# Transposing one granule's averages by DMA instead of TensorE, with an output tile moved ahead of its first FFN matmul

## Chip, cores, metric

One core of a Trainium2 chip. The metric is the device time of one execution in microseconds (us); a run is one such execution. The span of a profile is about 1.8 us shorter than the time of the same run.

## The reference, cut to what matters

```python
def _attn_ref(q, k, v, n_global, n_local):         # 4 batches, 8 heads, 768 tokens, 64 wide
    scores = scale * np.matmul(q, k.transpose(0, 1, 3, 2))
    keep = is_global | is_local                    # 8 global keys, a band of 96
    ...                                            # bias by distance, mask, softmax
    return np.matmul(a, v)

def _moe_ref(x, w_in, w_out, s, b):                # x: 3072 x 512, d_ff = 2048
    h = x @ w_in
    r = np.maximum(h, 0.0)
    g = s * (r * r) + b
    return g @ w_out

x = attn_out.transpose(0, 2, 1, 3).reshape(B * S, H * D)   # attention feeds the FFN
```

## The kernel before

The 3072 tokens are cut into 12 granules of 256. For each, attention gives the averages `xn` (tokens on partitions). They have to be transposed to `xT` (features on partitions) before the FFN's first product (L632 in the profile) can take them. After ReLU (ScalarE) and square (VectorE) the second product (L680, or for later granules the cheaper L968 and L832) gives the output. Everything is interleaved by hand in "steps": a step computes the score products of the next two units (L444; a unit is two heads of one granule), then the value products of its own two units (L504), with pieces of FFN work in between, so that TensorE has something to do while ScalarE and VectorE make the exponentials.

There are two ways to transpose the averages. Granules 0 to 3 use the first one, the others the second:

```python
    QK_PE = 4
    X_PE = 4
...
    def x_by_pe(j, evac=(nc.vector.tensor_copy, nc.scalar.copy)):
        t = xT_tile(j)
        nk = KC // len(evac)
        for e, ev in enumerate(evac):
            ps = ps_h.tile([P, nk, GT], BF16, name="ps_x", tag="psh")
            for kc in range(nk):
                for i in range(GB):
                    c = (e * nk + kc) * P
                    nc.tensor.transpose(          # L604: 8 for a granule
                        ps[:, kc, i * P : (i + 1) * P], xn[j][:, i, c : c + P], ident_bf[:]
                    )
            ev(t[:, e * nk : (e + 1) * nk, :], ps[:])     # L607: 2 copies from PSUM

    def x_by_dma(j):
        t = xT_tile(j)
        for i in range(GB):                       # L612: 2 for a granule, on SyncE's queue
            nc.sync.dma_start_transpose(t[:, :, i * P : (i + 1) * P], xn[j][:, i, :])
...
    def finish_granule(j):
        if j < X_PE:
            x_by_pe(j)
        else:
            x_by_dma(j)
        while stores:
            stores.pop(0)()
        if 6 <= j + LEAD < NJ:                    # later loads wait until this granule is done
            hold_loads(xT[j][0:1, 0, GT - 1 : GT])
            load_granule(j + LEAD)
```

Queries and keys of the granules from 4 on are also transposed by DMA (L363, four transposes of 128x512 a granule) on the same queue. The keys shifted by one block (`ko`) are copied from them by VectorE (L386, L387). The part of the order that the change touches:

```python
    qk_by_dma(5)                                  # granule 5's four transposes
    r0, q0 = p1_mm(2, 5)
    r0()
    stage_A(14)                                   # last values of granule 3
    stage_A(15, ps_h)
    q0()
    make_koff(4)                                  # the copies L386, L387
    run(p1[2][6:8])
    finish_granule(3)                             # the transposes in question
    run(scores(8))
    make_voff(4)
    p2_mm(2, 0, 0, FC // 2)
    emit_bvec()
    ...
    step(8, [lambda: rest(2, 0)] + late_p1(3, (0,)), late_p1(3, (1, 2)), late_p1(3, (3,)))
    step(
        9,
        [weight_sums[1]] + p2[2][1:2],
        [sg_sum(3)] + act_p1(3, (4, 5)),
        late_p1(3, (6,)) + [weight_sums[2]] + late_p1(3, (7,)) + [flush, sg_sum(1)],
    )
```

`late_p1(3, ...)` are pairs of FFN matmul groups of granule 3 (8 matmuls, then a ReLU, a square later); `rest` and `p2[2]` are granule 2's output tiles.

The softmax here doesn't subtract the row's maximum and nothing guards it: scores larger than these inputs give would overflow.

## Time and profile before

| before | value |
|---|---|
| time, median of the first 3 runs | 207.85 us (207.68 to 207.97) |
| span of the profile | 206.1 us |
| TensorE busy | 201.6 us |
| eight transposes of granule 3 (L604) | 0.45 us on TensorE |
| their copies out of PSUM (L607) | 0.42 us on VectorE, 0.58 us on ScalarE |

TensorE has hardly a gap, so the row to keep in mind is the 0.45 us: it is all that the change can gain. The lines of the profile that carry this are in the prediction.

### The profile page before, as it was taken

How to read it: one execution, taken by the hardware profiler on the slowest of the kernel's cores; microseconds unless marked ns; L12 is line 12 of the kernel's file. 1: busy time of each engine (PE TensorE's matmuls, PEld its weight loads, DVE VectorE, ACT ScalarE, POOL GpSimd, SP SyncE). 2: the span in 40 equal slices, each digit the busy share in tenths (PEclk: the TensorE clock that was granted, in tenths of full speed). 3: DMA queues.
4: the chain of work that ended last, by engine and by line, in shares of the span. 5: the costliest groups of instructions: out<-in, count | busy, mean ns of one | idle time of the engine just before them, and what ended most of it. 6: DMA issues, size and time to landing. Idle time of an engine off the chain costs nothing.

```text
span 206.1 us, 5375 instructions
## 1 busy us (share of the span) xinstructions
PE 201.6 (98%) x2209; PEld 162.5 (79%) x2214; DVE 164.8 (80%) x347; ACT 129.3 (63%) x200; POOL 70.2 (34%) x90
## 2 busy tenths in 40 slices
PE   8999999999999999999999999999999999999993
PEld 2678885557876588888888898888888889888883
DVE  6877689979989999999699865699866696737974
ACT  5767669585975668885763694763694754476200
POOL 8986333899555601808301908200000000000000
PEclk9999999999999999999999999999999999999999
DMA  5999999999999999999999999994360300340006
GB/s 156 177 178 201 207 206 180 155 153 131 126 143 125 156 125 229 117 168 188 145 272 192 131 173 202 180 192 78 54 207 3 101 4 0 69 138 0 3 7 197
DMA packets 110836, 28.17 MB, mean 137 GB/s; under 512 B 97852, under 2 KB 109308, under 8 KB 110812
## 3 DMA queue, kind: packets, MB, share of 16 engines
q0 software_dynamic: 76000, 13.11, 87.9%
q1 hardware_dynamic: 33612, 14.13, 39.9%
q10 hardware_dynamic: 1200, 0.59, 1.1%
q8 instruction: 17, 0.28, 0.5%
q14 instruction: 7, 0.06, 0.1%
HBM read 27.26 MB, written 6.29 MB: 163 GB/s over the span
## 4 chain that ended last, share of the span: by engine, by line
PE 95%; DMA 2%; DVE 0%; ACT 0%; issue 0%
PE ps L632 41%; PE ps L832 24%; PE ps L680 10%; PE ps_s L444 6%; PE ps_av L504 5%; PE ps L968 3%; DMA first<-in_k_dram 2%; PE ps_s L530 1%; PE ps_t L354 1%; PE ps_s L419 1%; PE ps_x L604 1%; PE ps_s L545 1%; PE ps_t L331 1%; PE ps_av L571 1%; PE ps_t L344 0%; PE ps_last L832 0%
## 5 line engine op out<-in xcount | busy, mean ns | idle before, releaser
L632 PE MATMUL ps<-xT,w_in_bf 128*128 128x256 bf16 x768 | 90.4, 273 | 0.0
L642 ACT ACTIVATE gT<-ps 128x512 bf16<-128x512 f32 x96 | 55.8, 598 | 46.0 <-PE ps L632 45.8
L632 PEld LDWEIGHTS <-w_in_bf 128*128 128x128 bf16 x768 | 73.0, 98 | 9.2 <-DVE xT L607 0.2
L453 ACT ACTIVATE pt<-ps_s 128x1024 bf16<-128x1024 f32 (+1 forms) x44 | 39.3, 946 | 2.9 <-PE ps_s L444 2.8
L832 PEld LDWEIGHTS <-gsum 128*128 128x128 bf16 x256 | 24.2, 98 | 3.7 <-DVE gsum L795 0.5
L460 DVE TENSOR_TENSOR pt<-pt,tmpl 128x1024 bf16<-128x1024 bf16 (+1 forms) x40 | 24.4, 644 | 2.1 <-ACT pt L453 2.0
L108 POOL DMA_DIRECT2D vb<-in_v_dram x24 | 21.6, 914 | 5.3 <-DMA w_out_bf<-in_moe_w_out_dram 3.3
L806 DVE TENSOR_TENSOR gT<-gT 128x1024 bf16<-128x1024 bf16 x20 | 13.7, 687 | 11.6 <-ACT gT L642 11.6
L680 PE MATMUL ps<-w_out_bf,gT 128*128 128x512 bf16 x91 | 21.8, 379 | 0.3
L469 DVE TENSOR_TENSOR xn<-ps_av,rc 128x256 bf16<-128x256 f32 x48 | 20.4, 425 | 1.7
L832 PEld LDWEIGHTS <-gT 128*128 128x128 bf16 x200 | 18.6, 98 | 2.3
L504 PEld LDWEIGHTS <-pt 128*128 128x128 bf16 x320 | 14.4, 97 | 2.8 <-DVE xn L469 0.9
L680 PEld LDWEIGHTS <-gT 128*128 128x128 bf16 x96 | 8.9, 98 | 9.6
L468 DVE RECIPROCAL rc<-ps_av 128x4 f32<-128x4 f32 x48 | 8.6, 179 | 9.1 <-PE ps_av L504 7.8
L504 PE MATMUL ps_av<-vb,pt 128*128 128x65 bf16 x208 | 15.5, 193 | 0.0
L832 PE MATMUL ps<-w_out_bf,gsum 128*128 128x256 bf16 x128 | 15.3, 273 | 0.0
L832 PE MATMUL ps<-wsub,gsum 128*128 128x256 bf16 x128 | 15.1, 273 | 0.0
L116 POOL DMA_DIRECT2D nat<-in_q_dram x14 | 12.5, 890 | 6.9 <-DMA nat<-in_q_dram 2.9
L645 DVE TENSOR_TENSOR gT<-gT 128x512 bf16<-128x512 bf16 x30 | 12.2, 421 | 3.2 <-ACT gT L642 2.7
L122 POOL COPY gate<-xT 1x1 bf16<-1x1 bf16 x6 | 1.9, 314 | 36.1 <-DMA xT<-xn 36.1
L116 POOL DMA_DIRECT2D nat<-in_k_dram x14 | 12.6, 900 | 4.7 <-DMA w_in_bf<-in_moe_w_in_dram 2.5
L832 PE MATMUL ps<-w_out_bf,gT 128*128 128x256 bf16 x120 | 13.9, 273 | 0.0
(124 smaller groups left out, 249.7 us busy)
## 6 DMA issues: line engine op xcount, KB each, us to landing
out_dram<-o_q SPq DMA_DIRECT2D x15, 256.0 KB, 2.6
vb<-in_v_dram POOLq DMA_DIRECT2D x24, 128.0 KB, 7.6
nat<-in_k_dram POOLq DMA_DIRECT2D x22, 128.0 KB, 6.8
nat<-in_q_dram POOLq DMA_DIRECT2D x22, 128.0 KB, 6.9
w_out_bf<-in_moe_w_out_dram POOLq DMA_DIRECT2D x4, 512.0 KB, 16.1
w_in_bf<-in_moe_w_in_dram POOLq DMA_DIRECT2D x4, 256.0 KB, 7.6
w_in_bf<-in_moe_w_in_dram POOLq DMA_DIRECT2D x2, 512.0 KB, 11.1
out_dram<-o_sb SPq DMA_DIRECT2D x4, 256.0 KB
```

Of the source, the lines that this page charges most:

```text
L108: nc.gpsimd.dma_start(vbuf[b % 2][:, sb, :, 0:D], rows_of(v, b, sb))
L116: nc.gpsimd.dma_start(t[:, n, i, :, :], rows_of(srcs[n], b, sb))
L444: nc.tensor.matmul(ps[:, hi, oc * P : (oc + 1) * P], lhsT=kt[rows], rhs=qt[rows], start=not bias, stop=not bias or part * GB + n == len(pl ...
L453: nc.scalar.activation(pt[:, :, 0:ncol], ps[:, :, 0:ncol], ACT.Exp, scale=QSCALE)
L460: nc.vector.tensor_tensor(pv, pv, m.rearrange("p h a c -> p h (a c)"), ALU.mult)
L469: nc.vector.tensor_tensor(dst, av[:, :, :, 0:D], rc[:].to_broadcast((P, 2, 2, D)), ALU.mult)
L504: nc.tensor.matmul(av[:, i, hi, 0 : D + 1], lhsT=pt[:, hi, c * P : (c + 1) * P], rhs=vv, start=(n == 0), stop=(n == len(terms) - 1),)
L632: nc.tensor.matmul(ps[:, i, :], lhsT=w_in_bf[:, kc, fc * P : (fc + 1) * P], rhs=xT[j][:, kc, :], start=(kc == 0), stop=(kc == KC - 1),)
L642: nc.scalar.activation(gs, ps[:], ACT.Relu)
L680: nc.tensor.matmul(po[:], lhsT=g_of(j)[:, fc, tb * P : (tb + 1) * P], rhs=w_out_bf[:, fc, :], start=(fc == 0), stop=(fc == FC - 1),)
L806: outs.append(lambda: nc.vector.tensor_tensor(gs, gs, gs, ALU.mult))
L832: nc.tensor.matmul(ps[:, tb, cs], lhsT=stat[:, fc, tb * P : (tb + 1) * P], rhs=mov[:, fc, cs], start=(fc == 0), stop=(fc == NH - 1),)
```

## The change

The intent: take granule 3's transposes off TensorE, which bounds the kernel, and leave them to the DMA engines. As a DMA transpose takes longer to arrive, the work that doesn't need it (all of granule 2's output) is moved ahead of granule 3's first FFN matmul.

```diff
-    X_PE = 4
+    X_PE = 3
@@ finish_granule
-            hold_loads(xT[j][0:1, 0, GT - 1 : GT])
+            hold_loads(g_of(2)[0:1, FC - 1, GT - 1 : GT] if j == 3 else xT[j][0:1, 0, GT - 1 : GT])
@@ steps 8 and 9
-    step(8, [lambda: rest(2, 0)] + late_p1(3, (0,)), late_p1(3, (1, 2)), late_p1(3, (3,)))
+    step(8, [lambda: rest(2, 0)], [lambda: p2_mm(2, 1, 0, FC // 2)], [lambda: rest(2, 1)])
     step(
         9,
-        [weight_sums[1]] + p2[2][1:2],
-        [sg_sum(3)] + act_p1(3, (4, 5)),
-        late_p1(3, (6,)) + [weight_sums[2]] + late_p1(3, (7,)) + [flush, sg_sum(1)],
+        late_p1(3, (0, 1)),
+        [weight_sums[2]] + late_p1(3, (2, 3)),
+        act_p1(3, (4, 5)) + [flush, sg_sum(3)] + late_p1(3, (6,)) + [weight_sums[1]] + late_p1(3, (7,)) + [flush, sg_sum(1)],
     )
```

The rest of the diff only joins two lines of step 10.

More of the change, by code (lines that the diff above doesn't have):

```diff
@@ L1285 @@
         [bias_diff, lambda: shifted_template(range(H)), sg_prod(5)],
-        [sg_sum(4)],
-        pre=[sg_sum(2)],
+        [sg_sum(4)], pre=[sg_sum(2)],
     )
```

## The prediction

> **What bounds the kernel now.** I read the page's first part, its slices and its chain first.
>
> ```profile
> span 206.1 us, 5375 instructions
> ...
> PE 201.6 (98%) x2209; PEld 162.5 (79%) x2214; DVE 164.8 (80%) x347; ACT 129.3 (63%) x200; POOL 70.2 (34%) x90
> ...
> DMA  5999999999999999999999999994360300340006
> ...
> PE 95%; DMA 2%; DVE 0%; ACT 0%; issue 0%
> ```
>
> TensorE is busy for 98% of the span and carries 95% of the chain that ended last. Nothing else holds the end. So work taken off TensorE shortens the run by its full length, and any new wait of TensorE lengthens it by its full length. The DMA row is the second thing to see: the DMA engines are at 9 tenths from the second slice (5 us each) to the 27th, so a transfer added at 60 us joins a full system.
>
> Then I read the chain in order of time around the change:
>
> ```profile
> 57.23 1.75 PE ps L632 x16
> 58.98 0.45 PE ps_x L604 x8
> 59.42 0.55 PE ps_s L444 x16
> 59.98 0.32 PE ps L680
> ...
> 67.73 0.87 PE ps L632 x8
> 68.61 0.55 PE ps_s L444 x16
> ```
>
> Columns: start, length, what. The eight transposes of granule 3 (L604) hold TensorE for 0.45 us; right after come the score products of step 8 (L444) and granule 2's output (L680).
>
> What the transposes' neighbour waits for is in the timeline of VectorE and of the weight loads:
>
> ```profile
> 59.24 0.18 DVE L387 COPY ko<-kx 128x64 bf16<-128x64 bf16 x1
> ...
> 59.54 0.27 PEld L444 LDWEIGHTS <-ko 64*128 64x128 bf16 x8
> ```
>
> The shifted keys ko of granule 4 are finished at 59.42, and the second half of L444 loads them at 59.54. There is only 0.12 us of slack between the two. The last transposed queries of granule 4 are just as close: issued at 49.34, 9.8 us to landing in the DMA view of that window, so there at 59.14, and L444 starts at about 59.36.
>
> Last, the issuing queue (SyncE) and what its transposes get from the DMA engines:
>
> ```profile
> 52.70 2.10 SPq L363 DMA_TRANSPOSE kx<-nat  x1
> 54.90 1.34 SPq L363 DMA_TRANSPOSE qx<-nat  x1
> 56.34 1.59 SPq L363 DMA_TRANSPOSE kx<-nat  x1
> 58.02 1.81 SPq L363 DMA_TRANSPOSE qx<-nat  x1
> 66.28 1.19 SPq L363 DMA_TRANSPOSE kx<-nat  x1
> ```
>
> Granule 5's four transposes are issued until 59.83, then the queue is free until 66.28: the hole that the new transposes will use. The DMA view of two windows (58.2 to 65.9, then 65.9 to 70.5) shows when those four move:
>
> ```profile
> q0 software_dynamic: 3712, 0.47, 121.0%
> q1 hardware_dynamic: 2283, 0.53, 57.8%
> ```
>
> ```profile
> q0 software_dynamic: 5606, 0.71, 241.3%
> ...
> q1 hardware_dynamic: 3, 0.00, 0.1%
> ```
>
> Columns: packets, MB, share. In the first window queue 1 carries about 4 x 512 packets of 256 bytes and the completion packets; in the second it is empty. So the four transposes, though issued from 52.70 on, move from 58.2 to 65.9, 1.93 us each, and the queue's work is done at 65.9.
>
> **What the Trainium skill says.** "TensorE: Matmul & The Clock Gate", Part 4: PE-mode transpose: it is a matmul whose output goes to PSUM, so a copy must follow; about 275 ns each in a kernel. The trace agrees on the copies (L607: 0.42 us on VectorE, 0.58 us on ScalarE), but eight in a row cost 0.45 us, 56 ns each, as they are pipelined; I use 0.45. "DMA: Bandwidth & Descriptors", SWDGE vs HWDGE vs iDMA: software and hardware queues feed different rings of each DMA engine, which takes them in turn. The trace agrees: from 59 to 63 us queue 0 moved 1794 packets and queue 1 1537, close to one for one, so a transpose has at most half of a busy engine's turns. Same page, Rules for kernel authors: issue a DMA early and wait for it late. That is what moving granule 2's output forward tries; the question is whether the distance suffices. "TensorE: Matmul & The Clock Gate", Why this matters for your kernels: idle gaps of more than about 3 us cost clock. The clock row of this trace is full throughout; the wait I expect is shorter, so I count no loss of clock.
>
> **The change part by part.** *Removed:* eight transposes, 0.45 us of TensorE on the path; two copies off the path. *Added:* two DMA transposes of granule 3's averages. The averages are ready at 58.37 (the last normalisation, 57.95 + 0.42), the queue is free at 59.83, so I expect the issues at 59.9 and about 61.2. *Moved:* the other half of granule 2's output (16 matmuls of 128x512) goes ahead of granule 3's first FFN matmul, so four FFN pairs that used to lie between now come later. No work is added, and the changes from one kind of matmul to another stay about as many. *Gate:* the loads of granule 7 wait for the last square of granule 2 (60.08 in this trace) in place of xT. The gate's copy ran at 61.75 only because the POOL queue reached it then, so nothing changes.
>
> Step 1, the saving at once. L444 could start at 58.98, but its queries land at 59.14 and ko is still finished at 59.42, as VectorE does that ahead of the copy that goes. With 0.06 us for the signal the second half of L444 starts at about 59.48 in place of 59.54 to 59.59. So of the 0.45 us only about 0.1 is left; the rest becomes a wait for ko and the queries. After L444 TensorE is at 59.90.
>
> Step 2, TensorE's arrival at granule 3's first FFN matmul. From 59.90: half an output tile 1.83, the bias vector 0.44, scores 0.55, the tile's other half 1.83, values (L504) 0.24, 1.75, 0.24, 1.75, scores 0.55, each as the chain has it. Sum 9.18, so 69.08. The same work of before, counted without moving anything, would stand at 59.42 + 0.55 + 9.18 = 69.15.
>
> Step 3, the landing of xT. Behind granule 5's transposes the two can move from 65.9. At the best pace (queue 1 moved 384 packets per us from 59 to 63, some 540 per transpose: 1.4 us) they end at 68.7, at the mean pace with its pauses (1.93 us) at 69.8. To the landing I add 0.8: granule 5's first two landed at 52.70 + 8.6 = 61.3 and 54.90 + 7.6 = 62.5, and by equal shares they ended at 60.1 and 62.1. So xT is there between 69.5 and 70.6; centre 70.0. Both blocks are needed, since the matmul takes 256 tokens.
>
> Step 4, the net. The FFN of granule 3 starts at 70.0 in place of the 69.15 that equals the pace of before: +0.85 us. The wait on TensorE itself is 0.9 us.
>
> Step 5, step 9 is denser. All eight FFN pairs of granule 3 fall in one step of about 8 us: ScalarE has eight evacuations of 0.60, two squares of 0.63 and two exponentials of 0.96 there, 8.0 us; VectorE has six squares, two weight differences of 1.21, a sum of 0.68, two normalisations of 0.6. The last squares, the sum for product 1 and 5, and the next masks end later relative to TensorE than now, and already now the values of unit 21 wait for the average before them (0.37 us at 81.09 in place of 0.24). I give 0.2 us for this, chosen low because TensorE's wait lets both engines catch up.
>
> Sum: +0.85 + 0.2 = +1.05 us on 207.85. Weighted with the case that xT is in time (below), I predict **208.7 us**.
>
> **The rivals.** *A: xT is in time.* Then the change is worth step 1's 0.1 us to at best 0.45 us: 207.4 to 207.8. For it: xT of granule 4 lands in 4.9 and 4.1 us, and from 59.9 and 61.2 that would be 66. Against: those two found the queue empty and the loads ending; at 60 us the transposes of granule 5 are ahead, with 8.6 and 7.6 us to landing. I give it 25%. *B: a long wait.* From the issue at 66.28 to the first packet of that transpose at about 70.5 the queue was empty and still took 4 us. If xT's descriptors come that slowly, or a pause as at 63.5 to 64.4 (10 GB/s) falls in, xT lands at 71 to 72: 209.7 to 210.5. I give it 15%. *C: the delay spreads.* Granule 6's loads and transposes go through the same engines, 1.5 us later at most; its queries landed at 78.8 and are needed at 81.5, so 2.7 us of slack and no new wait. *D: VectorE or ScalarE becomes the bound in step 9.* Step 5 made larger: up to 0.6 us, 208.5 even with xT in time.
>
> **Range and chances.** From 207.5 (A) to 209.9 (start of B). The three runs of before lie within 0.3 us, so noise is small. Faster by 2% would need 4.2 us and only 0.45 is removed; slower by 2% would need a wait of over 4 us. Faster 0.01, same 0.97, slower 0.02.
>
> **What would show it.** Right: SyncE issues two xT transposes at about 60 and 61; they land near 70; the first L632 of granule 3 follows a gap of about 0.9 us on TensorE whose releaser is the DMA of xT; L444 of step 8 starts hardly earlier than now, its second half bound by ko. Wrong: no gap ahead of L632 (step 3 fails, rival A); L444 a full 0.45 us earlier (step 1 fails); or a gap at the products after step 9 that is larger than the one ahead of L632 (step 5 and rival D).

## The result, and the profile after

| | median, us | range, us | runs |
|---|---|---|---|
| before | 207.78 | 207.67 to 207.97 | 6 |
| after | 209.28 | 208.42 to 210.08 | 6 |

The ratio is 1.0069 (95% interval 1.0043 to 1.0094): 0.7% slower, "same" at the 2% line. A ratio here is the mean time of one kernel's fast runs over that of the other's of the same rounds, so it is not quite the ratio of the medians. Two things stand out. The loss of 1.50 us by medians is more than all that could be gained. And the changed kernel's runs are spread over 1.66 us, where those of before lie within 0.30 us. The profile happens to be of its slowest run (210.08 us), which has to be remembered when its waits are read.

The page of the changed kernel (summary, chain and the group of the FFN's first product):

```profile
span 208.3 us, 5362 instructions
...
PE 201.6 (97%) x2201; PEld 161.9 (78%) x2206; DVE 164.9 (79%) x346; ACT 128.8 (62%) x199; POOL 70.2 (34%) x90
...
PE 82%; DMA 6%; DVE 5%; ACT 4%; SPq 1%; issue 1%
...
L632 PE MATMUL ps<-xT,w_in_bf 128*128 128x256 bf16 x768 | 90.1, 273 | 1.5 <-DMA xT<-xn 1.5
```

The eight matmuls are gone from the count (2209 to 2201), but the span is 2.2 us longer. TensorE's share of the chain that ended last fell from 95% to 82%, and the last line says for what: L632 waited 1.5 us for the DMA of xT. That column was 0.0 before. The chain in order of time (start, length, what) shows the path:

```profile
59.52 0.19 DVE ko L387
...
59.76 0.42 PE ps_s L444 x8
60.17 1.32 SPq L612
...
61.54 9.16 DMA xT<-xn
...
70.75 1.92 PE ps L632 x16
...
81.10 1.20 DVE pt L460 x2
...
82.43 0.44 DVE xn L469
...
82.91 0.41 PE ps_av L504 x8
```

There are three new places where something other than TensorE sets the pace: the shifted keys ko at 59.7, the landing of xT at 70.70 (9.16 us after the start of its second issue, at 61.54; the chain counts a DMA from there), and VectorE's normalisation ahead of unit 21's values at 82.9. SyncE's timeline shows the queue that xT shares:

```profile
52.41 1.32 SPq L363 DMA_TRANSPOSE kx<-nat  x1
...
58.10 1.96 SPq L363 DMA_TRANSPOSE qx<-nat  x1
60.16 4.01 SPq L612 DMA_TRANSPOSE xT<-xn  x2
```

Granule 5's transposes are issued up to 60.06 and xT's follow at once; between them there is no room. The DMA view of 66.1 to 69.6 us (packets, MB, share) shows xT's own passage (q1), with the load queue (q0, GpSimd's loads) beside it:

```profile
q0 software_dynamic: 2131, 0.27, 119.5%
q1 hardware_dynamic: 1096, 0.26, 60.8%
```

Two transposes are 1024 packets of 256 bytes; they took the 3.5 us of this window, about 1.75 us each.

**Where the 2.2 us are.** A table by stage can be read off TensorE's timeline at four marks: (a) the start of the 16 L632 just ahead of granule 3's transposes (57.07 before, 57.08 after), (b) the first L680 after step 8's scores (59.91, 60.08), (c) the first L444 of step 10 (76.63, 78.32), (d) the first L632 of granule 4 (82.72, 84.58); then to the end of VectorE's last result (203.26, 205.11) and from there to the end of the span. The stages hold the same TensorE work in both, but for the eight transposes in a to b. I use the same marks for the experiments.

| stage, us | before | after | difference |
|---|---|---|---|
| a to b: last transposes, step 8's scores | 2.84 | 3.00 | +0.16 |
| b to c: granule 2's output, granule 3's FFN | 16.72 | 18.24 | +1.52 |
| c to d: step 10 | 6.09 | 6.26 | +0.17 |
| d to VectorE's last result | 120.54 | 120.53 | 0.0 |
| from there to the end | 2.84 | 3.19 | +0.35 |

The sum is 2.2 us, the difference of the spans. Stage a to b is the one that should have become 0.45 us shorter. Why it did not is seen where VectorE and GpSimd are listed together, before:

```profile
58.07 0.88 POOL L108 DMA_DIRECT2D vb<-in_v_dram  x1
...
58.62 0.58 DVE L386 COPY ko<-kx 128x1024 bf16<-128x1024 bf16 x1
```

and after:

```profile
58.38 0.87 POOL L108 DMA_DIRECT2D vb<-in_v_dram  x1 [0.90 <-DMA vb<-in_v_dram]
...
58.63 0.85 DVE L386 COPY ko<-kx 128x1024 bf16<-128x1024 bf16 x1
```

The same copy started at the same time, but took 0.85 in place of 0.58 us, and in both it ended 0.23 to 0.25 us after GpSimd had finished writing a load's descriptors; the same copy with nothing beside it (at 57.25 in run 10) takes 0.42 us. The Trainium skill, "SBUF — State Buffer", SBUF: two separate sides, says that VectorE in its fast mode and GpSimd share a port pair under an exclusive lock for a whole instruction (that this copy runs in that mode is not shown here). The three durations agree with that, if the lock is taken and let go some 0.2 us after GpSimd's recorded start and end: at 66.78 in the changed kernel the next such copy started only 0.19 us after a write's recorded start, took 0.42 us, and it was the write that was longer (1.08 us). As GpSimd's loads are not timed against this copy, its end is a matter of chance.

The last stage, +0.35 us, is far from everything that was changed. SyncE's own waits show a difference there, before:

```profile
SPq L1383 <- DMA out_dram<-o_last: 0.6, 2, 0.3
...
SPq L1383 <- DMA out_dram<-o_q: 0.4, 1, 0.4
```

and after:

```profile
SPq L1382 <- DMA out_dram<-o_last: 1.4, 2, 1.3
```

(total, times, longest). The last stores themselves land after the same 1.9 us in both. At the end of the kernel SyncE waits one after another, in a fixed order, for the completion semaphores (the counters by which a DMA tells that it has landed). Those that SyncE's and ScalarE's DMAs carry are given out in turn, so with two more DMAs, xT's, the last stores carry other ones. The packed trace names them: before, the last store had the semaphore that is waited for last (118), and the waits ended with its landing; after, it has an early one (103), and six more waits of 0.06 us each follow its landing. That is 0.36 us.

### The profile page after: what moved, and what is told of

It reads as the page before. It is cut to its first block, busy times and chain, and to the rows that moved or that the text cites. A ratio compares the mean times of both kernels' runs of the same rounds, so it can differ in the third digit from the quotient of the medians.

```text
span 208.3 us, 5362 instructions
## 1 busy us (share of the span) xinstructions
PE 201.6 (97%) x2201; PEld 161.9 (78%) x2206; DVE 164.9 (79%) x346; ACT 128.8 (62%) x199; POOL 70.2 (34%) x90
## 4 chain that ended last, share of the span: by engine, by line
PE 82%; DMA 6%; DVE 5%; ACT 4%; SPq 1%; issue 1%
PE ps L632 36%; PE ps L832 24%; PE ps L680 7%; PE ps_av L504 4%; DMA xT<-xn 4%; PE ps_s L444 4%; DMA first<-in_k_dram 2%; ACT gT L642 2%; PE ps L968 1%; ACT pt L453 1%; DVE xn L469 1%; DVE pt L460 1%; PE ps_s L419 1%; DVE gT L645 1%; PE ps_s L530 1%; PE ps_t L354 1%
## 5 line engine op out<-in xcount | busy, mean ns | idle before, releaser
L632 PE MATMUL ps<-xT,w_in_bf 128*128 128x256 bf16 x768 | 90.1, 273 | 1.5 <-DMA xT<-xn 1.5
L632 PEld LDWEIGHTS <-w_in_bf 128*128 128x128 bf16 x768 | 73.1, 98 | 10.6 <-DMA xT<-xn 1.6
L680 PE MATMUL ps<-w_out_bf,gT 128*128 128x512 bf16 x91 | 21.8, 379 | 0.3
L504 PEld LDWEIGHTS <-pt 128*128 128x128 bf16 x320 | 14.4, 98 | 3.1 <-DVE xn L469 1.1
L680 PEld LDWEIGHTS <-gT 128*128 128x128 bf16 x96 | 8.8, 98 | 9.3
L504 PE MATMUL ps_av<-vb,pt 128*128 128x65 bf16 x208 | 15.4, 193 | 0.1
L122 POOL COPY gate<-xT 1x1 bf16<-1x1 bf16 x5 | 1.4, 282 | 36.4 <-DMA xT<-xn 36.4
```

The source lines that it names most:

```text
L504: nc.tensor.matmul(av[:, i, hi, 0 : D + 1], lhsT=pt[:, hi, c * P : (c + 1) * P], rhs=vv, start=(n == 0), stop=(n == len(terms) - 1),)
L632: nc.tensor.matmul(ps[:, i, :], lhsT=w_in_bf[:, kc, fc * P : (fc + 1) * P], rhs=xT[j][:, kc, :], start=(kc == 0), stop=(kc == KC - 1),)
L680: nc.tensor.matmul(po[:], lhsT=g_of(j)[:, fc, tb * P : (tb + 1) * P], rhs=w_out_bf[:, fc, :], start=(fc == 0), stop=(fc == FC - 1),)
```

## The experiments

The theory after the result: (T) moving the transposes to the queue puts xT behind granule 5's four, which themselves go at half pace beside the loads, and TensorE arrives before it; the order by itself is nearly free. The rivals: (O) the new order costs it, as the FFN of granule 3 is packed into one step and VectorE falls behind; (L) the latency of a DMA transpose costs it, whatever is ahead of it in the queue.

All kernels gave correct results. Times are medians, with range and number of runs; the ratio is against the kernel before in the same rounds (whose medians were 207.68, 207.80, 207.83 and 207.78 in the four batches). Against the changed kernel's interval of 1.0043 to 1.0094, those of runs 1, 7 and 9 lie wholly below. Those of 4, 5, 8 and 10 overlap it, so their gains on it are differences of medians that the times alone do not make sure. Landing times below are the last updates of xT's completion semaphores in the packed traces.

### 1. The new order alone

```diff
# against the changed kernel
-    X_PE = 3
+    X_PE = 4
```

> The new order alone, granule 3's averages still transposed on TensorE. Theory (the loss is TensorE's wait for the DMA transposes): no DMA wait is left, so 207.8 to 208.1 us, at most 0.3 us over the kernel before for the denser step 9. Rival (the new order itself costs, as eight FFN pairs crowd ScalarE and VectorE in one step): 209 us or more, close to the changed kernel's 209.28.

Measured: 207.96 us (207.73 to 208.17, 5), ratio 1.0010 (0.9998 to 1.0022). The profile has no wait for a DMA in steps 8 to 10; stages a to b and b to c are 2.84 and 16.72 us, exactly those of before. Only step 10 is longer, 6.56 us, in the slowest of its runs. So O is worth some 0.3 us of the 1.5. The end of the kernel is as before too (2.85 us from VectorE's last result).

### 2. The transposes by DMA in the old order

```diff
# against the kernel before
-    X_PE = 4
+    X_PE = 3
```

> The DMA transposes alone, in the old order, where granule 3's first FFN matmul stands at about 64.5 us. Theory (xT lands at about 70 us whatever TensorE does, set by the transposes ahead of it in the queue): TensorE waits 5 to 6 us there and nothing gives it back, 213 to 214 us. Rival (landing follows the issue by 4 to 5 us as for granule 4's xT, so at 65 to 66 us): 208.5 to 209.5 us.

Measured: 215.72 us (214.60 to 216.19, 4), ratio 1.0376 (1.0348 to 1.0405): slower. TensorE's timeline, and the row of granted clock on the page:

```profile
69.43 1.89 PE L632 MATMUL ps<-xT,w_in_bf 128*128 128x256 bf16 x8 [5.12 <-DMA xT<-xn]
```

```profile
PEclk9999999999998599999999999999999999999999
```

TensorE came to granule 3's FFN 5.12 us before xT did, yet xT landed at 69.38, no later than in the changed kernel (70.70). So its landing does not depend on when it's wanted. The move of granule 2's output is worth 6.4 us (215.72 - 209.28), the loss of clock included: without it the change would be a clear loss. The time was 2 us above what I expected: the clock fell to 8 and 5 tenths in two slices, the mean to 0.984, and eight L632 took 1.89 us, where the other kernels need 1.04. The wait of 1.45 us in the changed kernel left its clock at 9 throughout. This agrees with the limit that the prediction quotes from the Trainium skill.

### 3. The two scalar loads taken out of the queue at the start

Ahead of granule 5's transposes, the queue also carries s and b, broadcast to 128 partitions: 256 packets of four bytes. In the changed kernel's DMA view, 57.4 to 58.7 us, queue 1 shows

```profile
q1 hardware_dynamic: 512, 0.05, 62.4%
```

512 packets but only 0.05 MB: by size, half of them are these. They hold the queue for about 1 us (by the trace's packet records 57.5 to 58.6).

```diff
+    load_scalars()          # right after the first FFN groups, at the program's start
...
     qk_by_dma(4)
-    load_scalars()
```

> The changed kernel with the loads of the two scalars s and b issued before granule 4's transposes instead of between those of granules 4 and 5: their 256 packets of 4 bytes leave the queue ahead of the transposes. Theory (one queue worked off in order, a packet per turn): at 384 packets per us they hold it 0.7 us, so xT lands 0.5 to 1 us earlier and the run takes 208.4 to 208.8 us. Rival (a fixed latency from issue to landing, or the pace of issuing): no change, 209.3 us.

Measured: 209.52 us (208.82 to 210.92, 6), ratio 1.0094. A miss by the experiment's own fault: the small packets now came among the first loads; L504 waited 0.57 us for the first values at 11.29, and mark a stands at 57.74 in place of 57.08. Its profile shows no wait for xT, but as two things changed at once it decides nothing. Run 7 repeats it in a better place.

### 4. Granule 5's transposes taken off the queue

The four transposes that stand ahead of xT are done by TensorE instead. It costs 16 TensorE transposes, twice what the change saved.

```diff
-    qk_by_dma(5)
     r0, q0 = p1_mm(2, 5)
...
-    step(8, [lambda: rest(2, 0)], [lambda: p2_mm(2, 1, 0, FC // 2)], [lambda: rest(2, 1)])
+    step(
+        8,
+        [lambda: rest(2, 0), lambda: qk_wide(5, 0, cp)],
+        [lambda: p2_mm(2, 1, 0, FC // 2), lambda: qk_wide(5, 1, acp)],
+        [lambda: rest(2, 1)],
+    )
```

> The changed kernel with granule 5's keys and queries transposed on TensorE in step 8 (16 transposes, 0.9 us more TensorE work) instead of by DMA ahead of xT in the queue. Theory (xT waits behind granule 5's transposes): xT lands at 64 to 66 us, before it is needed, the wait of 0.9 to 1.5 us goes and 0.9 us of work comes: 208.5 to 208.9 us, faster than the changed kernel in spite of more work on the bound engine. Rival (the wait is not due to the queue, or the order costs): 209.8 to 210.3 us.

Measured: 208.67 us (208.65 to 208.85, 5), ratio 1.0047 (1.0035 to 1.0059). SyncE's timeline:

```profile
58.16 2.52 SPq L612 DMA_TRANSPOSE xT<-xn  x2
```

xT's packets moved from 62.5 to 66.4 by the trace's records, xT landed at 67.77 (later than the 64 to 66 expected), and L632 started at 69.60 with no wait. With more work on TensorE, this kernel's median is 0.6 us below the changed one's, and its runs lie within 0.2 us where those lay within 1.66. So the four transposes ahead are what made xT late, and the times scatter less without them. But L is not refuted. The DMA view of 58.5 to 62.4 us has nothing on queue 1:

```profile
q0 software_dynamic: 4684, 0.59, 240.0%
q8 instruction: 1, 0.02, 2.1%
```

On this empty queue xT's first packet still came 4.3 us after the start of its first issue (58.16), and the two transposes landed 7.4 and 8.4 us after the starts of theirs, where the changed kernel has 8.9 and 9.2. (That is beside a full load queue; at 162.42, with no load moving, a transpose of xT lands after 2.4 us in the same kernel.) The second one landed 2.93 us earlier than there. Of this, 2.14 us is that SyncE, without the four issues before it, could issue it earlier (59.40 in place of 61.54), and 0.79 us that it took less time from there. Stage b to c is 17.61 us, 0.89 above before: the 16 transposes and nothing else.

### 5. More work put ahead of xT

Both value groups of step 9 (L504, 0.5 us) come ahead of granule 3's FFN.

```diff
     step(
         9,
-        late_p1(3, (0, 1)),
-        [weight_sums[2]] + late_p1(3, (2, 3)),
-        act_p1(3, (4, 5)) + ...
+        [],
+        [],
+        late_p1(3, (0, 1)) + [flush, weight_sums[2]] + late_p1(3, (2, 3)) + [flush] + act_p1(3, (4, 5)) + ...
+        pool=ps_h,
     )
```

> The changed kernel with both value products of step 9 (L504, 0.48 us) ahead of granule 3's first FFN matmul. Theory (xT lands at a time of its own; every microsecond of other work ahead of it is hidden): the wait falls by 0.4 to 0.5 us: 208.7 to 209.0 us. Rival (the wait moves along with TensorE's order): no change, 209.3 us.

Measured: 208.84 us (208.16 to 209.43, 6), ratio 1.0043 (1.0021 to 1.0064): as expected. In the profiled run, the second longest, L632 started at 70.07 after a wait of 0.43 us for xT. The landing near 70 again, and less waiting before it: 0.5 us of work put ahead of the landing took 0.44 us off the loss, by medians of different batches. (The edit also moves the points where squares are flushed and takes another PSUM pool.)

### 6. The scalars on another queue (and two kernels built on it)

```diff
     def load_scalars():
-        nc.sync.dma_start(s_bc[:], moe_s.to_broadcast((P, 1)))
-        nc.sync.dma_start(b_bc[:], moe_b.to_broadcast((P, 1)))
+        nc.scalar.dma_start(s_bc[:], moe_s.to_broadcast((P, 1)))
+        nc.scalar.dma_start(b_bc[:], moe_b.to_broadcast((P, 1)))
...
     template(range(H))
+    load_scalars()
...
     qk_by_dma(4)
-    load_scalars()
```

> The changed kernel with the loads of the two scalars issued at about 30 us from ScalarE's queue, so that neither the start of the kernel (as in the run with early scalars, whose first values then came 0.6 us late) nor the transposes' queue has their packets. Theory (the queue is worked off in order, its 256 packets of 4 bytes took a turn each at 57.5 to 58.6 us): granule 5's transposes and xT move 0.7 to 1 us earlier, TensorE's wait for xT falls by as much: 208.3 to 208.7 us. Rival (pace or latency of issuing): 209.3 us.

Together with the edit of run 5 and VectorE's weight difference moved to step 8:

> Scalars off the queue, value products first, and one weight difference (1.2 us of VectorE) moved from the dense step 9 into step 8. Theory: xT's wait of 0.5 to 1.5 us is covered (1.2 us gained), and the wait of unit 21's values for the average before them (0.43 us in the run with the order alone) goes: 207.6 to 207.9 us, as the kernel before. Rival: still over 208.5 us.

And with the copy of the shifted keys earlier as well:

> The same, and granule 4's shifted keys ko copied ahead of granule 3's last averages instead of behind them, so that step 8's score products no longer wait for them. Theory (most of the 0.45 us saved was turned into a wait for ko): 0.2 to 0.3 us faster than without this, 207.3 to 207.6 us, the first version under the kernel before. Rival (the queries of granule 4, landing at about 59.1 us, hold it as much): no gain.

Measured: 225.83 us (225.16 to 226.35, 5), 226.18 us (225.71 to 226.60, 4) and 226.32 us (226.09 to 227.14, 4); ratios 1.086 to 1.089. All three share one fault, which ScalarE's timeline of the first shows:

```profile
53.27 1.04 ACT L253 COPY tmpl<-tmpl 128x1024 bf16<-128x1024 bf16 x1 [17.78 <-DMA kx<-nat]
```

The second scalar load, issued from ScalarE, was given a completion semaphore that a transpose of granule 4 was using, so its issue (52.73) and all of ScalarE stood still for 17.78 us until that transpose had landed. These three say nothing on the question, except how dear a shared completion semaphore can be (and something on the kernel's end, below).

### 7. The scalars on the same queue, but at 30 us

Now they stay on SyncE's queue, but are issued where it is empty. A memset of their tiles by VectorE keeps them from going earlier.

```diff
     run(p1[0][7:8])
+    nc.vector.memset(s_bc[:], 0.0)
+    nc.vector.memset(b_bc[:], 0.0)
+    load_scalars()
...
     qk_by_dma(4)
-    load_scalars()
```

> Third try at taking the scalars' 256 packets out from between the transposes: SyncE issues them alone at about 28 us (they wait for a small fill of their tiles), after the start and long before granule 4's transposes, and no other engine's queue is involved. Theory (queue worked off in order): granule 5's transposes and xT move 0.7 to 1 us earlier, the wait for xT falls by as much: 208.3 to 208.7 us. Rival (pace or latency of issuing): 209.3 us.

Measured: 208.39 us (208.08 to 208.80, 5), ratio 1.0027 (1.0015 to 1.0040): as expected, and 0.9 us less than the changed kernel (209.28 in an earlier batch). By the trace's packet records xT's last packet left at 67.8 in place of 69.5; xT landed at 68.45, and L632 started at 69.07 with no wait. Stage b to c is 16.77, against 16.72 before. So the loss in that stage (1.52 us in the changed kernel's profile) was the wait for xT, and what stands ahead of xT made it. The edit takes the two loads out of the queue and their issues, 0.6 us each, off SyncE, so that xT's issue starts at 59.31 in place of 60.16; this run does not tell these two apart.

What is left in this profile: a to b is 3.02 (a wait for the last queries, 0.23 us, where the saving should be), c to d is 6.60 (unit 21's values wait 0.46 us for VectorE), and the end is 3.17.

### 8. Scalars early, values first, and a weight difference moved

```diff
# scal_sp, with run 5's edit, weight_sums[1] taken out of step 9, and
-    step(8, [lambda: rest(2, 0)], [lambda: p2_mm(2, 1, 0, FC // 2)], [lambda: rest(2, 1)])
+    step(8, [lambda: rest(2, 0)], [lambda: p2_mm(2, 1, 0, FC // 2), weight_sums[1]], [lambda: rest(2, 1)])
```

> Scalars as in the run just named, value products of step 9 first (these alone gave 208.84), and one weight difference of VectorE moved out of the dense step. Theory: the wait for xT is covered and the one for unit 21's average gone: 207.6 to 207.9 us, as the kernel before. Rival: over 208.4 us.

Measured: 208.60 us (208.34 to 209.06, 5), ratio 1.0044 (1.0031 to 1.0057). A miss, no faster than run 7. TensorE's timeline shows two waits for VectorE in place of those removed:

```profile
59.55 0.40 PE L444 MATMUL ps_s<-qx,ko 64*128 64x128 bf16 x8 [0.44 <-DVE ko L387]
...
73.73 3.65 PE L632 MATMUL ps<-xT,w_in_bf 128*128 128x256 bf16 x32 [0.33 <-DVE xn L469]
```

### 9. The shifted keys earlier too

```diff
# the kernel of run 8, and
     qk_by_dma(5)
+    make_koff(4)
     r0, q0 = p1_mm(2, 5)
...
     q0()
-    make_koff(4)
```

> The same, and granule 4's shifted keys copied ahead of granule 3's last averages. Theory (most of the 0.45 us saved had turned into a wait for ko): 0.2 to 0.3 us faster than without, 207.3 to 207.6 us, under the kernel before. Rival (granule 4's last queries hold step 8's scores as much): no gain.

Measured: 208.16 us (208.06 to 208.79, 6), ratio 1.0027 (1.0014 to 1.0040). It misses what I expected, but is 0.44 us faster than run 8. Stage a to b is 2.40 us, 0.44 less than before: here, for the first time, the whole gain of the eight transposes shows. So the prediction's step 1 had the right cause. (Of the two medians alone this can't be said: the intervals of runs 8 and 9 overlap.) The copy now started 0.13 us ahead of GpSimd's descriptors and took 0.42 us, and the small one after it took 0.53 us (0.18 elsewhere), ending with GpSimd's (58.22 and 58.24), as the lock would have it. But TensorE now comes earlier to an xT that is not earlier: in its longest, profiled run L632 at 69.94 waited 0.63 us for it.

### 10. The same with the load queue held back

If the transposes are slow because they share the DMA engines with the loads, then they should go faster when granule 6's loads are held until granule 2's squares are done (about 60 us).

```diff
# the kernel of run 9, and
-        if 6 <= j + LEAD < NJ:
+        if 7 <= j + LEAD < NJ:
             hold_loads(...)
+            if j == 3:
+                load_granule(6)
             load_granule(j + LEAD)
```

> The last version with one thing more: the loads of granule 6, issued from 51 us on, are held until granule 2's squares are done (about 60 us). Theory (the transposes are slow because each of their packets waits a turn of the loads'): from 52 to 61 us the load queue runs dry, the transposes of granule 5 go at up to twice the pace, xT lands at 67 to 68.5 us instead of about 70, and no wait for it is left: 207.5 to 207.9 us. A later wait for granule 6's keys would show at about 82 us and is possible. Rival (the pace of the transposes is their own): xT lands at about 70 as before, 208.2 us.

Measured: 208.29 us (208.18 to 209.00, 6), ratio 1.0031 (1.0013 to 1.0049). The DMA view of 63 to 65.4 us has one queue only:

```profile
q1 hardware_dynamic: 808, 0.20, 129.9%
```

In run 9 queue 1 moved 343 packets in that window, beside 618 of the loads. xT's last packet left at 65.6 in place of 69.0 (the trace's packet records), xT landed at 67.02, and no wait for xT is left in this profile. So the transposes' pace is set by sharing with the loads, which was step 3's basis. But the time did not fall, and the 207.5 to 207.9 us expected were missed. Stage b to c is 17.07: TensorE ends step 9's scores at 68.74, and then

```profile
69.01 0.20 PE L504 MATMUL ps_av<-vb,pt 128*128 128x65 bf16 x1 [0.28 <-DVE xn L469]
```

it waits for VectorE. What comes next in line behind xT is VectorE's normalisation, and behind that the end of the kernel.

### The stages of all of them

| us | a to b | b to c | c to d | end | median time |
|---|---|---|---|---|---|
| before | 2.84 | 16.72 | 6.09 | 2.84 | 207.78 |
| order alone (1) | 2.84 | 16.72 | 6.56 | 2.85 | 207.96 |
| changed kernel | 3.00 | 18.24 | 6.26 | 3.19 | 209.28 |
| granule 5 on TensorE (4) | 2.79 | 17.61 | 6.26 | 2.94 | 208.67 |
| values first (5) | 2.77 | 17.32 | 6.26 | 3.16 | 208.84 |
| scalars at 30 us (7) | 3.02 | 16.77 | 6.60 | 3.17 | 208.39 |
| 8 | 3.01 | 17.44 | 6.26 | 3.19 | 208.60 |
| 9 | 2.40 | 17.52 | 6.26 | 3.19 | 208.16 |
| 10 | 2.39 | 17.07 | 6.27 | 3.21 | 208.29 |

The stages are of one profiled run each, and in 1, 7, 8, 9 and the changed kernel of the longest of its runs; only the medians compare kernels. (In 5, a further 0.38 us lies between d and the end.) The column "end" splits in two: 2.84 to 2.94 where SyncE and ScalarE together issue as many DMAs as before or two fewer, 3.16 to 3.21 in every kernel where they issue two more. In run 6's three kernels SyncE alone issues as many as before (the scalars went to ScalarE), and the end is 3.2 us: the count of both matters.

None of these beats the kernel before. In run 10, a to b gains 0.45 us, and b to c (+0.35), c to d (+0.18) and the end (+0.37) give back 0.90.

## Why the prediction was right

**The sum.** 208.7 us was predicted with a range of 207.5 to 209.9; 209.28 was measured, within the range and 0.6 above the centre. Unweighted, the steps gave 208.9; the 0.35 us of the missing term below is about what separates this from the measurement, and the range of 2.4 us took it in. All other terms of the mechanism were there.

**Step 1 (only 0.1 of the 0.45 us is left)** was right in its cause and wrong in size, even in sign: a to b became 0.16 us longer, not 0.1 shorter. L444's second half was bound by ko, as it said, but started at 59.76, 0.17 later than before, not 0.1 earlier. The copy that makes ko was assumed to end when it had ended before; it took 0.27 us longer beside GpSimd's descriptors. Run 9 shows the cause: with ko earlier the stage is 0.44 us shorter. The error cost the sum little, because TensorE waited for xT afterwards anyway.

**Step 2 (TensorE arrives at 69.08)**: L444's last matmul ended at about 69.3 in the changed kernel, 0.2 late by step 1. Right.

**Step 3 (xT lands at 69.5 to 70.6, behind granule 5's transposes)**: 70.70 in the profiled run, which is the slowest of six, so just outside. Its parts hold: xT took about 1.75 us for each transpose beside the loads, run 4 shows that xT is in time without the four ahead (though most of the time from issue to landing, 7.4 to 8.4 us, is there on an empty queue too, which the prediction has under rival B alone), run 10 that the sharing sets the pace, and run 2 that the landing does not depend on when it is wanted. What the step left out is how much the landing varies from one execution to the next: the times of the changed kernel are spread over 1.66 us, where the step's range for the landing is 1.1 us wide. Nor did it see that 256 small packets were among what stood ahead; the queue's end at 65.9, on which it built, contained them, and run 7 took them away. (They moved until 58.9, so the four transposes of before took 1.75 us each from there, not 1.93 from 58.2.)

**Step 4 (net +0.85, a wait of 0.9)**: in the profiled run, marks a to c together are +1.68 and the wait 1.45 us. For the median run there is no profile; taking step 10 and the end as constant, an estimate is 1.50 - 0.17 - 0.35 = 1.0 us, near the step's value.

**Step 5 (a denser step 9, +0.2)**: +0.17 in step 10 in the changed kernel, at the place named, unit 21's values. Run 1 gives 0.28 us for the order alone.

**The term that was missing** is the end of the kernel, +0.35 us. The prediction followed only the part of the kernel that the diff touches and took everything after granule 4 as unchanged. That d to VectorE's last result is equal to 0.01 us confirms that, but SyncE's waits after it were not thought of. Two more DMAs turn the completion semaphores round, and six waits of 0.06 us come to stand behind the last store's landing: this is read off the trace's semaphores. `X_PE` alone switches it in either order (2.84 before, 3.19 in run 2; 2.85 in run 1, 3.19 in the changed kernel). No run changed the semaphores and nothing else.

**The rivals.** A (xT in time) is what run 7 shows when the queue is freed; the fastest run of the changed kernel, 208.42, is 0.64 above before, about the 0.16 + 0.17 + 0.35 of the other stages, so it probably had little wait. B (a landing at 71 to 72) did not come about in the profiled run, the slowest of the six (70.70), though its time of 210.08 lies in B's range. C (the delay spreads) is ruled out by the stage from d to VectorE's last result. D (VectorE as the bound) stayed small here, but is the next wait in line once xT is in time (runs 8 and 10).

## What to carry to other kernels

Moving work from the bounding engine to a DMA pays only if it lands before the engine comes. Count the landing from when the issuing engine can issue it, with the time that such a DMA takes on an empty queue (7.4 to 8.4 us here beside the loads), and add the packets that are ahead of it; look for what shares the queue, small packets too. Ahead of that, look for the second-latest input at the place where the time is to be saved: an operand with 0.1 us of slack turns a saving of 0.45 us into a wait. And follow a change to the queue's last waits, as a different number of DMAs can change which of them comes last.

## What the Trainium skill lacked or had wrong

- "DMA: Bandwidth & Descriptors", Latency and other measured facts, gives an effective rate of 261 GB/s for DMA transposes (with a non-contiguous middle dimension; more when contiguous); a 128x512 block of bf16 (131 KB) would then take 0.5 us (an estimate from it). Here its packets took about 1.75 us beside a busy load queue. The page has no figure for a transpose that shares the engines, and none for a transpose from issue to landing: 8.9 and 9.2 us behind four others, 7.4 and 8.4 us on an empty queue beside loads, 2.4 us without them (run 4).
- "TensorE: Matmul & The Clock Gate", Part 4: PE-mode transpose: about 275 ns each in a kernel; here one lasted 0.22 us, and eight in a row took 0.45 us, 56 ns each, sixteen 0.89 in run 4. The page has no figure for a row of them.
- "SBUF — State Buffer", SBUF: two separate sides: the lock fits (a VectorE copy of 0.42 us took 0.58 and 0.85 us beside a GpSimd descriptor write of 0.87 us), but not as counted from the profiler's records: a copy that started 0.19 us after a write's recorded start was not held (66.78 in the changed kernel).
- No page read for this case gives the time that a completion semaphore shared between the DMAs of two engines can cost: ScalarE stood still for 17.78 us.
- Nor does any say that the waits at a kernel's end depend on which completion semaphore the last store carries: 2.84 us where it is waited for last, 3.16 to 3.21 us where six waits follow it.
